# Attention rewritten in transposed form, two heads at a time, and issued between the feed-forward chunks

## The chip, the cores and the metric

One core of a Trainium2 chip. The metric is device time in microseconds (us) of one execution. Timed runs of a single core agree here within about 1.5%, and all times below are medians. Each profile is one execution, so its span differs by a few us from the timed runs. A ratio is the mean time of one kernel's fast runs over the mean of the other's of the same rounds, so it is not quite the ratio of the medians that are quoted.

## The reference, cut to what matters

```python
# q, k, v: (4 batches, 8 heads, 768 positions, 64), fp32
scores = (q @ k.T) / 8
keep = (column < 4) | ((row - column >= 0) & (row - column < 128))   # 4 sink keys, window 128
a = exp(scores where keep), each row divided by its sum
x = (a @ v) as (3072 tokens, 512)
out = (relu(x @ w_gate) * (x @ w_val)) @ w_out                        # 512 -> 1536 -> 512
```

## The kernel before

The attention handles one head and 128 queries at a time. Queries and keys are loaded as fp32 through SyncE and transposed on TensorE; v is loaded with a cast to bf16 by GpSimd, one load per head.

```python
for b in range(B):
    for h in range(H):
        nc.sync.dma_start(out=qL[:], in_=q[b, h].rearrange("(n p) d -> p n d", p=128))
        nc.sync.dma_start(out=kL[:], in_=k[b, h].rearrange("(n p) d -> p n d", p=128))
        for t in range(nqt):                       # 6 tiles, fp32 transposes of q and k
            nc.tensor.transpose(tp[:, :], qL[:, t, :], ident[:, :]); # ... copy, the same for k
        nc.gpsimd.dma_start(out=vA[:, :, :D], in_=v[b, h].rearrange("(n p) d -> p n d", p=128))
        for qt in range(nqt):
            # per key tile (sinks as a tile of 4): scores 128x128, Exp, mask, value matmul
            # then reciprocal, scale, fp32 transpose, copy, store to a temporary in memory
```

The feed-forward starts when all attention is done: it loads its weights, then per 256 tokens reloads the transposed attention from the temporary, and runs 12 steps of gate and value matmuls (256 columns) and 24 output matmuls (512 columns).

The softmax here doesn't subtract the row's maximum and nothing guards it: scores larger than these inputs give would overflow.

Of the kernel before, what the change touches and what calls it, by code (L numbers as in the profile page):

```python
# [8 lines left out]
F32 = mybir.dt.float32  # L9
BF16 = mybir.dt.bfloat16  # L10
Alu = mybir.AluOpType
Act = mybir.ActivationFunctionType


@with_exitstack
def kernel(
# [12 lines left out]
    nc = tc.nc  # L29
    B, H, S, D = q.shape  # L30
    n_sink = 4
    window = 128
    assert D == 64 and S % 128 == 0
    QT = 128
    nqt = S // QT
    scale = 1.0 / (D ** 0.5)

    d_model = moe_w_gate.shape[0]
    d_ff = moe_w_gate.shape[1]
    n_tokens = B * S  # L40
    assert d_model == H * D

    xT = nc.dram_tensor("xT_tmp", (d_model, n_tokens), F32, kind="Internal").ap()

    const = ctx.enter_context(tc.tile_pool(name="const", bufs=1))
    ident = const.tile([128, 128], F32)
    make_identity(nc, ident)

    m_causal_sink = const.tile([128, 128], BF16)
    m_strict_sink = const.tile([128, 128], BF16)  # L50
    m_causal = const.tile([128, 128], BF16)
    for m, op, cm, st in ((m_causal_sink, Alu.is_ge, -1, 1), (m_strict_sink, Alu.is_gt, 1, -1), (m_causal, Alu.is_ge, -1, 1)):
        nc.gpsimd.memset(m[:], 1.0)
        nc.gpsimd.affine_select(out=m[:], in_=m[:], compare_op=op, fill=0.0,
                                base=0, pattern=[[st, 128]], channel_multiplier=cm)
    nc.gpsimd.memset(m_causal_sink[0:n_sink, :], 1.0)
    nc.gpsimd.memset(m_strict_sink[0:n_sink, :], 1.0)
    m_strict = const.tile([128, 128], BF16)
    nc.gpsimd.memset(m_strict[:], 1.0)
    nc.gpsimd.affine_select(out=m_strict[:], in_=m_strict[:], compare_op=Alu.is_gt, fill=0.0,  # L60
                            base=0, pattern=[[-1, 128]], channel_multiplier=1)

    attn_ctx = ExitStack()
    qkpool = attn_ctx.enter_context(tc.tile_pool(name="qk", bufs=3))
    vpool = attn_ctx.enter_context(tc.tile_pool(name="vp", bufs=3))
    spool = attn_ctx.enter_context(tc.tile_pool(name="sp", bufs=4))
    ps_s = attn_ctx.enter_context(tc.tile_pool(name="ps_s", bufs=2, space=bass.MemoryType.PSUM))
    ps_av = attn_ctx.enter_context(tc.tile_pool(name="ps_av", bufs=2, space=bass.MemoryType.PSUM))
    ps_t = attn_ctx.enter_context(tc.tile_pool(name="ps_t", bufs=2, space=bass.MemoryType.PSUM))
    opool = attn_ctx.enter_context(tc.tile_pool(name="op", bufs=3))  # L70

    for b in range(B):
        for h in range(H):
            qL = qkpool.tile([128, nqt, D], F32)
            kL = qkpool.tile([128, nqt, D], F32)
            nc.sync.dma_start(out=qL[:], in_=q[b, h].rearrange("(n p) d -> p n d", p=128))
            nc.sync.dma_start(out=kL[:], in_=k[b, h].rearrange("(n p) d -> p n d", p=128))
            qT = qkpool.tile([D, nqt, 128], BF16)
            kT = qkpool.tile([D, nqt, 128], BF16)
            for t in range(nqt):  # L80
                tp = ps_t.tile([D, 128], F32)
                nc.tensor.transpose(tp[:, :], qL[:, t, :], ident[:, :])  # L82
                nc.vector.tensor_copy(qT[:, t, :], tp[:, :])  # L83
                tp = ps_t.tile([D, 128], F32)
                nc.tensor.transpose(tp[:, :], kL[:, t, :], ident[:, :])  # L85
                nc.vector.tensor_copy(kT[:, t, :], tp[:, :])  # L86
            vA = vpool.tile([128, nqt, D + 1], BF16)
            nc.gpsimd.dma_start(out=vA[:, :, :D], in_=v[b, h].rearrange("(n p) d -> p n d", p=128))  # L88
            nc.vector.memset(vA[:, :, D], 1.0)

            for qt in range(nqt):
                if qt == 0:
                    kts = [(0, 128, m_causal_sink)]
                elif qt == 1:
                    kts = [(0, 128, m_strict_sink), (1, 128, m_causal)]
                else:
                    kts = [(0, n_sink, None), (qt - 1, 128, m_strict), (qt, 128, m_causal)]

                av = ps_av.tile([128, D + 1], F32)
                first = True  # L100
                for ki, (ktidx, ksz, mask) in enumerate(kts):
                    s_ps = ps_s.tile([128, 128], F32)
                    nc.tensor.matmul(  # L103
                        out=s_ps[:ksz, :128],
                        lhsT=kT[:, ktidx, :ksz],
                        rhs=qT[:, qt, :],
                        start=True, stop=True,
                    )
                    e = spool.tile([128, 128], BF16)
                    nc.scalar.activation(e[:ksz, :], s_ps[:ksz, :], Act.Exp, bias=0.0, scale=scale)  # L110
                    if mask is not None:
                        nc.vector.tensor_tensor(e[:ksz, :], e[:ksz, :], mask[:ksz, :], op=Alu.mult)  # L112
                    last = ki == len(kts) - 1
                    nc.tensor.matmul(  # L114
                        out=av[:, :], lhsT=e[:ksz, :], rhs=vA[:ksz, ktidx, :],
                        start=first, stop=last,
                    )
                    first = False

                osb = opool.tile([128, D], F32)  # L120
                rcp = opool.tile([128, 1], F32)
                nc.vector.reciprocal(rcp[:, :], av[:, D:D + 1])  # L122
                nc.vector.tensor_scalar(osb[:, :], av[:, :D], rcp[:, :], None, op0=Alu.mult)  # L123
                ot_ps = ps_t.tile([D, 128], F32)
                nc.tensor.transpose(ot_ps[:, :], osb[:, :], ident[:, :])  # L125
                ot = opool.tile([D, 128], F32)
                nc.vector.tensor_copy(ot[:, :], ot_ps[:, :])  # L127
                nc.sync.dma_start(
                    out=xT[h * D:(h + 1) * D, b * S + qt * 128: b * S + qt * 128 + 128],
                    in_=ot[:, :],  # L130
                )

    attn_ctx.close()
    KI = 128
    ko_m = d_model // KI
    ff_m = d_ff // KI

    wpool = ctx.enter_context(tc.tile_pool(name="wpool", bufs=1))
    wg = wpool.tile([KI, ko_m, d_ff], BF16)
    wv = wpool.tile([KI, ko_m, d_ff], BF16)  # L140
    wo = wpool.tile([KI, ff_m, d_model], BF16)
    nc.gpsimd.dma_start(out=wg[:], in_=moe_w_gate.rearrange("(ko ki) n -> ki ko n", ki=KI))
    nc.gpsimd.dma_start(out=wv[:], in_=moe_w_val.rearrange("(ko ki) n -> ki ko n", ki=KI))
    nc.gpsimd.dma_start(out=wo[:], in_=moe_w_out.rearrange("(ko ki) n -> ki ko n", ki=KI))

    xpool = ctx.enter_context(tc.tile_pool(name="xpool", bufs=3))
    hpool = ctx.enter_context(tc.tile_pool(name="hpool", bufs=2))
    ps_g = ctx.enter_context(tc.tile_pool(name="ps_g", bufs=1, space=bass.MemoryType.PSUM))
    ps_o = ctx.enter_context(tc.tile_pool(name="ps_o", bufs=1, space=bass.MemoryType.PSUM))
    orpool = ctx.enter_context(tc.tile_pool(name="orpool", bufs=3))  # L150

    TOK = 256
    ntt = n_tokens // TOK
    TG = TOK // 128

    for tt in range(ntt):
        xt = xpool.tile([KI, ko_m, TOK], BF16)
        nc.gpsimd.dma_start(
            out=xt[:],
            in_=xT.rearrange("(ko ki) t -> ki ko t", ki=KI)[:, :, tt * TOK: (tt + 1) * TOK],  # L160
        )
        hT = hpool.tile([KI, ff_m, TOK], BF16)
        for m in range(ff_m):
            gp = ps_g.tile([KI, TOK], F32)
            vp = ps_g.tile([KI, TOK], F32)
            for ko in range(ko_m):
                nc.tensor.matmul(out=gp[:], lhsT=wg[:, ko, m * KI:(m + 1) * KI],  # L167
                                 rhs=xt[:, ko, :], start=ko == 0, stop=ko == ko_m - 1)
            for ko in range(ko_m):
                nc.tensor.matmul(out=vp[:], lhsT=wv[:, ko, m * KI:(m + 1) * KI],  # L170
                                 rhs=xt[:, ko, :], start=ko == 0, stop=ko == ko_m - 1)
            gs = hpool.tile([KI, TOK], F32)
            nc.scalar.activation(gs[:], gp[:], Act.Relu, bias=0.0, scale=1.0)  # L173
            nc.vector.tensor_tensor(hT[:, m, :], gs[:], vp[:], op=Alu.mult)  # L174
# [43 lines left out]
```

## Time and profile before

| | before |
|---|---|
| device time | 621.58 us (621.3 to 621.86) |
| TensorE busy | 565.2 us, 91% of the span |
| GpSimd busy | 40.3 us, 7% |
| attention, weight hole, feed-forward | about 390, 28 and 202 us |

A group's line in the profile gives the source line, the engine, the operation, what it writes and reads, the count, then busy us and mean ns of one, then the us that the engine sat idle just before these instructions and what ended most of that. The slices cut the span in 40 equal parts, each digit being the busy share in tenths. The lines themselves stand in the prediction.

### The profile page before, as it was taken

How to read it: one execution, taken by the hardware profiler on the slowest of the kernel's cores; microseconds unless marked ns; L12 is line 12 of the kernel's file. 1: busy time of each engine (PE TensorE's matmuls, PEld its weight loads, DVE VectorE, ACT ScalarE, POOL GpSimd, SP SyncE). 2: the span in 40 equal slices, each digit the busy share in tenths (PEclk: the TensorE clock that was granted, in tenths of full speed). 3: DMA queues.
4: the chain of work that ended last, by engine and by line, in shares of the span. 5: the costliest groups of instructions: out<-in, count | busy, mean ns of one | idle time of the engine just before them, and what ended most of it. 6: DMA issues, size and time to landing. Idle time of an engine off the chain costs nothing.

```text
span 619.8 us, 9768 instructions
## 1 busy us (share of the span) xinstructions
PE 565.2 (91%) x2976; PEld 299.5 (48%) x2976; DVE 331.2 (53%) x1512; ACT 185.8 (30%) x625; POOL 40.3 (7%) x63
## 2 busy tenths in 40 slices
PE   6899999999999999999999998069999999999996
PEld 2344444444444444444444444036667766666664
DVE  4666666666666666667666666113333433333332
ACT  3333333332333333333333333012222222222221
POOL 3100101010010001001000000100000000000000
PEclk9999999999999999999999999999999999999999
DMA  8333235533323323333332300692121122222000
GB/s 125 53 54 73 50 59 83 90 50 53 73 49 58 72 50 59 58 61 52 55 73 50 58 16 16 121 194 51 35 52 32 40 51 52 51 53 52 35 35 34
DMA packets 103075, 36.80 MB, mean 59 GB/s; under 512 B 78960, under 2 KB 98928, under 8 KB 103024
## 3 DMA queue, kind: packets, MB, share of 16 engines
q0 software_dynamic: 34032, 11.01, 16.6%
q1 hardware_dynamic: 68992, 25.18, 16.0%
q8 instruction: 23, 0.38, 0.3%
q14 instruction: 28, 0.23, 0.1%
HBM read 34.60 MB, written 12.58 MB: 76 GB/s over the span
## 4 chain that ended last, share of the span: by engine, by line
PE 80%; DVE 11%; DMA 5%; issue 2%; ACT 2%; POOL 0%; SPq 0%; POOLq 0%; DVEq 0%; ACTq 0%
PE s_ps L103 15%; PE vp L170 11%; PE op L178 10%; PE gp L167 10%; PE tp L82 10%; PE av L114 8%; PE ot_ps L125 8%; PE tp L85 7%; DMA wo<-in_moe_w_out_dram 4%; DVE qT L83 3%; DVE e L112 2%; DVE rcp L122 2%; DVE ot L127 2%; ACT e L110 2%; DVE kT L86 1%
## 5 line engine op out<-in xcount | busy, mean ns | idle before, releaser
L110 ACT ACTIVATE e<-s_ps 128x128 bf16<-128x128 f32 (+1 forms) x480 | 129.2, 275 | 256.4 <-PE s_ps L103 120.4
L103 PE MATMUL s_ps<-qT,kT 64*128 64x128 bf16 (+1 forms) x480 | 127.0, 275 | 2.8 <-ACT e L110 2.6
L174 DVE TENSOR_TENSOR hT<-gs,vp 128x256 bf16<-128x256 f32 x144 | 60.5, 420 | 115.4 <-PE vp L170 115.4
L173 ACT ACTIVATE gs<-gp 128x256 f32<-128x256 f32 x144 | 55.4, 384 | 168.2 <-PE gp L167 154.9
L167 PE MATMUL gp<-xt,wg 128*128 128x256 bf16 x576 | 88.4, 276 | 14.8 <-DMA wg<-in_moe_w_gate_dram 13.8
L114 PE MATMUL av<-vA,e 128*128 128x65 bf16 (+1 forms) x480 | 95.5, 239 | 6.3 <-DVE e L112 5.2
L82 PE MATMUL tp<-ident,qL 128*64 128x128 f32 x192 | 80.6, 420 | 15.6 <-DVE qT L83 8.4
L170 PE MATMUL vp<-xt,wv 128*128 128x256 bf16 x576 | 87.3, 274 | 4.0 <-DMA wv<-in_moe_w_val_dram 3.2
L178 PE MATMUL op<-wo,hT 128*128 128x512 bf16 x288 | 87.2, 379 | 2.0 <-DMA wo<-in_moe_w_out_dram 0.8
L85 PE MATMUL tp<-ident,kL 128*64 128x128 f32 x192 | 80.4, 419 | 4.6 <-DVE kT L86 0.9
L127 DVE COPY ot<-ot_ps 64x128 f32<-64x128 f32 x192 | 52.7, 280 | 47.7 <-PE ot_ps L125 43.9
L103 PEld LDWEIGHTS <-kT 64*128 64x128 bf16 (+1 forms) x480 | 44.6, 94 | 69.5 <-issue 49.1
L114 PEld LDWEIGHTS <-e 128*128 128x128 bf16 (+1 forms) x480 | 46.5, 106 | 61.9 <-issue 27.5
L170 PEld LDWEIGHTS <-wv 128*128 128x128 bf16 x576 | 56.0, 97 | 40.5 <-issue 26.8
L125 PE MATMUL ot_ps<-ident,osb 128*64 128x128 f32 x192 | 74.0, 419 | 0.8 <-DVE osb L123 0.8
L83 DVE CAST qT<-tp 64x128 bf16<-64x128 f32 x192 | 53.3, 277 | 32.8 <-PE tp L82 28.0
L167 PEld LDWEIGHTS <-wg 128*128 128x128 bf16 x576 | 56.9, 99 | 25.2 <-issue 16.0
L86 DVE CAST kT<-tp 64x128 bf16<-64x128 f32 x192 | 53.0, 276 | 23.0 <-PE tp L85 22.4
L123 DVE TENSOR_SCALAR osb<-av,rcp 128x64 f32<-128x64 f32 x192 | 50.9, 273 | 0.0
L82 PEld LDWEIGHTS tp<-ident,qL 128*64 128x64 f32 x192 | 24.6, 128 | 53.4 <-DVE qT L83 31.3
L88 POOL DMA_DIRECT2D vA<-in_v_dram x32 | 26.4, 824 | 317.7 <-DVE rcp L122 272.2
L122 DVE RECIPROCAL rcp<-av 128x1 f32<-128x1 f32 x192 | 31.2, 165 | 24.1 <-PE av L114 22.5
(30 smaller groups left out, 185.9 us busy)
## 6 DMA issues: line engine op xcount, KB each, us to landing
qL<-in_q_dram SPq DMA_DIRECT2D x32, 192.0 KB, 2.8
kL<-in_k_dram SPq DMA_DIRECT2D x32, 192.0 KB, 3.0
xT_tmp<-ot SPq DMA_DIRECT2D x192, 32.0 KB, 1.9
out_dram<-ot SPq DMA_DIRECT2D x24, 256.0 KB, 2.0
vA<-in_v_dram POOLq DMA_DIRECT2D x32, 96.0 KB, 3.3
xt<-xT_tmp POOLq DMA_DIRECT2D x12, 256.0 KB, 4.3
wg<-in_moe_w_gate_dram POOLq DMA_DIRECT2D x1, 1536.0 KB, 10.5
wv<-in_moe_w_val_dram POOLq DMA_DIRECT2D x1, 1536.0 KB, 17.1
```

What stands on the lines that cost most here:

```text
L82: nc.tensor.transpose(tp[:, :], qL[:, t, :], ident[:, :])
L83: nc.vector.tensor_copy(qT[:, t, :], tp[:, :])
L85: nc.tensor.transpose(tp[:, :], kL[:, t, :], ident[:, :])
L103: nc.tensor.matmul(out=s_ps[:ksz, :128], lhsT=kT[:, ktidx, :ksz], rhs=qT[:, qt, :], start=True, stop=True,)
L110: nc.scalar.activation(e[:ksz, :], s_ps[:ksz, :], Act.Exp, bias=0.0, scale=scale)
L114: nc.tensor.matmul(out=av[:, :], lhsT=e[:ksz, :], rhs=vA[:ksz, ktidx, :], start=first, stop=last,)
L125: nc.tensor.transpose(ot_ps[:, :], osb[:, :], ident[:, :])
L127: nc.vector.tensor_copy(ot[:, :], ot_ps[:, :])
L167: nc.tensor.matmul(out=gp[:], lhsT=wg[:, ko, m * KI:(m + 1) * KI], rhs=xt[:, ko, :], start=ko == 0, stop=ko == ko_m - 1)
L170: nc.tensor.matmul(out=vp[:], lhsT=wv[:, ko, m * KI:(m + 1) * KI], rhs=xt[:, ko, :], start=ko == 0, stop=ko == ko_m - 1)
L174: nc.vector.tensor_tensor(hT[:, m, :], gs[:], vp[:], op=Alu.mult)
L178: nc.tensor.matmul(out=op[:], lhsT=hT[:, m, tg * 128:(tg + 1) * 128], rhs=wo[:, m, :], start=m == 0, stop=m == ff_m - 1)
```

## The change

The intent is to take the attention off TensorE's time: fewer and wider matmuls, no fp32 transposes, no trip of the result through memory, and the attention of the next batch done between the feed-forward chunks of this one. Keys lie in tiles of 128; every second tile has the 4 sink keys in its first 4 rows and 124 keys of its own. Everything is loaded as bf16 with a cast during the load, tile by tile, through GpSimd. The value tile carries columns of ones, so the value matmul also gives the sums; these go through memory to be inverted in a compact layout and to come back broadcast. The core of the diff, with cuts marked by "...":

```diff
-            nc.sync.dma_start(out=qL[:], in_=q[b, h].rearrange("(n p) d -> p n d", p=128))
-            nc.sync.dma_start(out=kL[:], in_=k[b, h].rearrange("(n p) d -> p n d", p=128))
...
-            nc.gpsimd.dma_start(out=vA[:, :, :D], in_=v[b, h].rearrange("(n p) d -> p n d", p=128))
...
+ROW0 = [0, 124, 252, 376, 504, 628, 752]
...
+    def load_q(b, p, ts, slot):
+        for t in ts:
+            nc.gpsimd.dma_start(out=qn[slot][:, t, :, :], in_=rows(q, b, p, t * 128, 128))
+
+    def load_kv(b, p, js, slot):
+        for x, dst in ((k, kn[slot]), (v, vn[slot])):
+            for j in js:
+                r0 = ROW0[j]
+                lo, hi = (4, 128) if j in (1, 3, 5) else ((0, 16) if j == 6 else (0, 128))
+                nc.gpsimd.dma_start(out=dst[lo:hi, j, :, 0:64], in_=rows(x, b, p, r0 + lo, hi - lo))
+                if j in (1, 3, 5):
+                    nc.gpsimd.dma_start(out=dst[0:4, j, :, 0:64], in_=rows(x, b, p, 0, 4))
...
+    def st_T(s, qts, js):        # stage T: bf16 transposes of q and k of two heads, copies
...
+    def st_S(s, g):              # stage S: scores of up to 507 columns per head, Exp, mask
...
+    def st_V(s, half, oab):      # stage V: value matmuls with the sums, copy
...
+    def norm(b, p, oab, q0, n, d1, d2):
+        nc.sync.dma_start(out=dd.rearrange("(o h s) -> o h s", o=1, h=2), in_=oab[64:65, :, q0:q0 + n])
+        nc.sync.dma_start(out=dc[0:pp, 0:cc], in_=dd.rearrange("(p c) -> p c", c=cc))
...          # d1 chunks later: reciprocal, store, broadcast load; d2 later: two multiplies
+            for m in range(FM):
+                ci = bi * FM + m
+                want = (ci + 1) * 5 // 2 if ci < 17 else 42 + (ci - 16) * 24 // 24
+                while si < min(total, want):
+                    for L in load_at.pop(si, []):
+                        L()
+                    stages[si]()
+                    si += 1
+                tick()
+                chunk(b, c0, n, m)
```

A "pair" below is two heads of one batch, 16 in all; a full pair takes 26 loads: 12 of 128 rows, 6 of 124, 6 of 4 (the sinks) and 2 of 16. Batch 0 is done in halves, the first half of all four pairs before the first chunk. A "chunk" is one step of gate and value matmuls, 96 in all.

## The prediction

> **What bounds the kernel now.** I read the page first, then the chain of waits, then a table of stretches, then the groups by form. From the page:
>
> ```profile
> span 619.8 us, 9768 instructions
> PE 565.2 (91%) x2976; PEld 299.5 (48%) x2976; DVE 331.2 (53%) x1512; ACT 185.8 (30%) x625; POOL 40.3 (7%) x63
> ...
> PE   6899999999999999999999998069999999999996
> ...
> PE 80%; DVE 11%; DMA 5%; issue 2%; ACT 2%; POOL 0%; SPq 0%; POOLq 0%; DVEq 0%; ACTq 0%
> PE s_ps L103 15%; PE vp L170 11%; PE op L178 10%; PE gp L167 10%; PE tp L82 10%; PE av L114 8%; PE ot_ps L125 8%; PE tp L85 7%; DMA wo<-in_moe_w_out_dram 4%; DVE qT L83 3%; DVE e L112 2%; DVE rcp L122 2%; DVE ot L127 2%; ACT e L110 2%; DVE kT L86 1%
> ```
>
> TensorE is occupied nearly throughout, and the chain that sets the end is 80% TensorE. The slices show two phases with a hole between them, near 390 to 418 us: the wait for the feed-forward weights (their load is 4% of the chain). Two stretches tell the phases apart (columns: stretch, its length, then busy time and count of PE, PEld, DVE, ACT, POOL, then clock, DMA share, GB/s):
>
> ```profile
> 200.00:300.00 100.00, 93.58 (x401) 41.60 (x400) 66.72 (x352) 33.34 (x125) 6.54 (x8) 1.00 0.34 58
> 430.00:520.00 90.00, 89.97 (x644) 62.06 (x643) 33.66 (x75) 24.92 (x65) 3.70 (x5) 1.00 0.22 50
> ```
>
> In attention, TensorE starts only 4.0 matmuls per us, in the feed-forward 7.2, and those are the wider ones. So attention (about 390 us) is not arithmetic: it is many short matmuls and fp32 transposes, each separated by hand-offs. The feed-forward is dense. In the chain listed in order of time, the bursts of twelve output matmuls start at 445.19, 462.01 and 478.83 us: 16.82 us per 256 tokens, 202 us for twelve. Its columns are 12 x (96 x 256 + 24 x 512) = 442,368[...].
>
> The second thing to see is an engine that is idle now, GpSimd, because the change gives it work. The groups by form:
>
> ```profile
> L88 POOL DMA_DIRECT2D vA<-in_v_dram x32 | 26.4, 824 | 317.7 <-DVE rcp L122 272.2 <-PE av L114 22.3 <-PE s_ps L103 12.1
> L158 POOL DMA_DIRECT2D xt<-xT_tmp x12 | 8.9, 744 | 165.1 <-PE vp L170 160.5 <-DVE e L112 2.3 <-DMA xT_tmp<-ot 2.2
> L144 POOL DMA_DIRECT2D wo<-in_moe_w_out_dram x1 | 1.0, 1037 | 0.0
> L142 POOL DMA_DIRECT2D wg<-in_moe_w_gate_dram x1 | 0.8, 752 | 38.4 <-DMA xT_tmp<-ot 38.4
> ```
>
> One issue of a casting load takes GpSimd 0.74 to 1.04 us, hardly depending on bytes (256 KB and 1536 KB: both about 0.75). Two of them back to back show that this is occupancy and not latency:
>
> ```profile
> 4.10 1.66 POOL L88 DMA_DIRECT2D vA<-in_v_dram  x2
> ```
>
> [...] wo is 1.04 us on GpSimd and 24.4 us to landing. [...] in the changed kernel every q, k and v load, fp32 to bf16, is on that engine. In the kernel before, q and k go by SyncE. [...] Twelve output matmuls of N = 512 take 2.66 us in the chain, 222 ns each [...].
>
> **The change part by part.**
>
> *TensorE work.* Removed: 384 fp32 transposes of q and k (161 us busy), 192 of the output (74), 480 score matmuls (127), 480 value matmuls (95.5). Added per pair of heads and batch, 16 times: 13 bf16 transposes of 128 columns, 2 x 1417 score columns, 2 x 1417 value columns, in all 7,332 columns [...] my estimate is 3.9 us. Feed-forward: 96 chunks of 8 matmuls of about 384 columns [...], with 3 output matmuls each (0.67) [...]: 2.04 us per chunk, 96 x 2.04 = 196 us. Sum: 196 + 16 x 3.9 = 258 us. If TensorE alone bound it, with a prologue of some 50 us in place of part of the attention, and a tail of 10, the end would be near 305 us.
>
> *VectorE and ScalarE.* ScalarE rows give 278 ns at 128 elements and 384 at 256, so 0.83 ns per element: per pair 2.9 us of Exp, 0.9 of copies of kT, 1.6 of outputs, and 6 chunks x 0.49; with the output copies 9.3 us per pair. VectorE at about 1.05 ns per element (420 at 256): some 10 us. Both lie well below the 16 us that TensorE needs per pair (6 x 2.04 + 3.9), so both are beside it.
>
> *GpSimd.* Fit the four rows by contiguous source runs (v 768, xt 512, wo 1536, wg 512): 0.598 us + 0.29 ns per run fits all within 10 ns. A 128-row load of two heads has 256 runs: 0.67 us. A pair needs 26 loads: 18 big ones (18 x 0.67 = 12.06), 6 sink loads of 8 runs (3.6), 2 of 32 runs (1.2): 16.9 us. That is more than TensorE's 16. Splitting one load of 768 runs (0.82) into three or more is what costs.
>
> *The path that sets the end.* GpSimd in order: first halves of the four pairs of batch 0, 4 x 7.23, with 3.5 us of constants and start: 32 us. Eight weight quarters: issue 6 us, but the built program lets only eight loads be outstanding (each waits for the landing of the eighth before), and the weights, 4.7 MB in 24.4 us before, give 2.0 us per quarter; so the next eight loads wait, and GpSimd is 7 us late. Second halves 4 x 9.65: about 85 us. Output weights and their waits: 93 us. Then 12 pairs x 16.9 = 203: the last load is issued at 296 us less a little overlap, and lands 3.3 us later as v does now: T of the last pair starts near 297 us. In the changed program's order, 56 of the 96 chunks stand before it. After it: 40 chunks x 2.04 = 82 us, the last pair's attention 4 us, 36 output matmuls left at the end 8 us, a copy and a store 2.5 us. Sum: 297 + 96.5 = 393 us by trace.
>
> TensorE could not have been later: its chunks 0 to 55 and fourteen pairs are some 170 us of work after a start near 50 us. It waits for loads. The 28 us weight hole disappears in the prologue; the store of the transposed attention to memory and its reload vanish from the path too.
>
> **The rivals.**
>
> *A: loads cost less, TensorE binds.* If the fixed 0.6 us shrinks for small shapes, the steady state becomes TensorE's 16.1 us per pair and only the first part still waits for loads. For it: the fit is extrapolated from 512 runs down to 8. With 20% cheaper loads the third batch starts near 140 us, then 81 chunks x 2.04, 8 pairs x 3.9 and the tail give 348. With no waiting at all about 305.
>
> [...]
>
> *C: the transfers bind.* Between 100 and 380 us the casting queue shows 18,832 packets at 14.4% of 16 engines, 34 ns each. A pair has 4,672 runs, 292 per engine, 9.9 us: less than 16.9. It is hidden unless landing exceeds eight issues (5.4 us).
>
> *D: the normalisation round trip (four transfers of about 2 us on SyncE, with the VectorE waiting in order) stalls a chunk.* It is placed some five chunks (over 10 us) ahead; I give it a few us at most.
>
> **Range and chances.** The base sum is 393, halfway towards A pulls it down, B pushes it up; I take 386, range 340 to 420. A result over 600 would need the fixed cost of a load to double, so faster is nearly certain: 0.98.
>
> **What would show it.** Right: GpSimd busy 70% or more with DMA issues of about 0.67 us; TensorE busy under 75%, its largest idle before the transposes, released by loads of q (the last of each pair); the GpSimd work ending near 300 us, after which TensorE is dense; each late chunk 2.04 us. A is right if GpSimd has gaps and q is not what TensorE waits for; B if the 124-row issues are longer than the 128-row ones; C if loads take over 5.4 us to land and GpSimd waits for landings; D if the transposed output's multiply sits on the chain. The prediction is wrong above all if an issue of a small load costs much less, or more, than 0.6 us.

The feed-forward came to 2.04 us per chunk: 0.67 for the three output matmuls, from the 222 ns of the trace, and the rest in two terms. The 3.9 us for a pair of heads is like the 2.04 an estimate; the 16 us per pair, 258, 305, 348 and the 393 us of the whole are made with both. By the trace alone, the feed-forward before took 202 us for 442,368 columns, 2.19 columns per ns; at that rate a chunk of 4,608 columns takes 2.10 us and the 7,332 columns of a pair 3.35. Rival B was that the 124-row loads cost more than those of 128 rows; it came to 0.88 us for each and 413 us in all. The 1.05 ns per element of VectorE is an estimate as well: the groups by form give 165 ns at 1 element, 276 to 280 at 128 and 420 at 256, so 1.0 to 1.1 per element between them. The limit of eight outstanding loads can be seen in the trace of the changed kernel: after the eight weight loads (40.30 to 46.3 us), loads two to eight that follow wait 0.60 to 1.67 us each, for wv and wg in turn, and the ninth for a load of k.

## The result, and the profile after

The changed kernel takes 465.17 us (463.48 to 466.86) against 621.58: ratio 0.748, 95% interval 0.742 to 0.755. It is much faster, but 79 us slower than the 386 predicted, and outside the range of 340 to 420.

From the page of the changed kernel, the lines that answer to those of before:

```profile
span 465.0 us, 5011 instructions
PE 292.8 (63%) x1752; PEld 170.9 (37%) x1752; DVE 143.7 (31%) x280; ACT 140.8 (30%) x225; POOL 349.6 (75%) x439
...
PE   0033320564062818254959798897969699999996
...
POOL 8999499995999999999999999999999400000000
PEclk9999999988557676695979897989889799999999
...
POOL 61%; PE 23%; DMA 9%; issue 6%; ACT 0%; POOLq 0%; ACTq 0%
POOL vn L92 20%; POOL kn L92 17%; POOL qn L85 13%; PE op L265 8%; PE gp L246 7%; PE vp L252 7%; POOL vn L94 5%; POOL kn L94 4%; DMA kn<-in_k_dram 3%; DMA wo<-in_moe_w_out_dram 2%; DMA qn<-in_q_dram 2%; DMA vn<-in_v_dram 1%; PE ops L181 1%; POOL wg L99 1%; POOL wv L99 1%
```

TensorE's busy time fell from 565 to 293 us, so the work did go. But the chain that ended last was 80% TensorE and is now 61% GpSimd, all of it loads (L92, L94 and L85 load q, k and v, L99 the weights). GpSimd is nearly full for 31 slices but two, and where it stops TensorE becomes dense. The table of stretches says the same (stretch, length, then busy time and count of PE, PEld, DVE, ACT, POOL, clock, DMA share, GB/s):

```profile
86.00:365.00 279.00, 183.49 (x1145) 110.12 (x1145) 92.74 (x167) 96.64 (x148) 271.95 (x336) 0.81 0.68 62
365.00:465.00 100.00, 93.70 (x529) 51.60 (x528) 30.47 (x53) 32.59 (x60) 0.94 (x2) 0.97 0.15 45
```

Between 86 and 365 us GpSimd is busy 97% of the time, TensorE 66%. The groups by form show what a load costs, and what TensorE waits for:

```profile
L92 POOL DMA_DIRECT2D kn<-in_k_dram x112 | 107.4, 968 | 10.5 <-DMA wo<-in_moe_w_out_dram 4.8 <-DMA wv<-in_moe_w_val_dram 2.9 <-DMA wg<-in_moe_w_gate_dram 1.3
...
L85 POOL DMA_DIRECT2D qn<-in_q_dram x96 | 69.6, 744 | 1.8 <-DMA vn<-in_v_dram 1.1 <-issue 0.7
...
L94 POOL DMA_DIRECT2D kn<-in_k_dram x48 | 28.4, 591 | 1.2 <-DMA wg<-in_moe_w_gate_dram 0.6 <-DMA wv<-in_moe_w_val_dram 0.6
...
L144 PE MATMUL tps<-ident,qn 128*128 128x128 bf16 x96 | 23.0, 263 | 126.6 <-DMA qn<-in_q_dram 115.3 <-POOL ident masks.py:199 11.0
```

TensorE idles 115 us for q, which is the last load of each pair. GpSimd itself waits for almost nothing. L92 mixes forms, so its 968 ns is a mean; the GpSimd timeline in the steady part separates them (start, time, then the merged instructions):

```profile
254.11 4.34 POOL L85 DMA_DIRECT2D qn<-in_q_dram  x6
258.44 2.05 POOL L92 DMA_DIRECT2D kn<-in_k_dram  x2
260.48 0.60 POOL L94 DMA_DIRECT2D kn<-in_k_dram  x1
```

A 128-row load takes 4.34 / 6 = 0.72 us. The two of L92 are one of 128 and one of 124 rows, so the 124-row load takes 2.05 - 0.73 = 1.32 us, nearly twice as long for fewer bytes. A sink load of 4 rows takes 0.59. A pair thus takes 12 x 0.73 + 6 x 1.32 + 6 x 0.59 + 2 x 0.51 = 21.2 us of GpSimd; the chain shows the q loads of successive pairs starting at 127.0, 148.1, 169.2 and 190.3 us, a step of 21.1.

The granted clock was 0.81 on the mean of the stretch from 86 to 365 us. It does not set the pace there: GpSimd's waits, 16 us in the whole span, are for landings of earlier loads and for its own issue, none for TensorE. In the experiment "resident" below, where TensorE is dense from 110 us on, the clock is 0.98 to 1.00; when it falls is not worked out here. The 1.00 that the views show at the start of a run is no measurement. The clock entries of the trace begin at 90.0 us in the changed kernel, and the views count what lies before as full; yet four gate matmuls of 380 columns take 1.47 us at 87.23 and 0.80 at 92.54. In the kernel before, the entries begin only at 414.5 us: four of 256 columns take 1.04 us at 413.56 and 0.60 at 415.19. That its attention ran at a lowered clock as well is my estimate from these two times; no record shows it.

### The profile page after: what moved, and what is told of

Its sections match the earlier page's. It is cut to its first block, busy times and chain, and to the rows that moved or that the text cites. A ratio compares the mean times of both kernels' runs of the same rounds, so it can differ in the third digit from the quotient of the medians.

```text
span 465.0 us, 5011 instructions
## 1 busy us (share of the span) xinstructions
PE 292.8 (63%) x1752; PEld 170.9 (37%) x1752; DVE 143.7 (31%) x280; ACT 140.8 (30%) x225; POOL 349.6 (75%) x439
## 3 DMA queue, kind: packets, MB, share of 16 engines
q0 software_dynamic: 160944, 14.61, 47.5%
## 4 chain that ended last, share of the span: by engine, by line
POOL 61%; PE 23%; DMA 9%; issue 6%; ACT 0%; POOLq 0%; ACTq 0%
POOL vn L92 20%; POOL kn L92 17%; POOL qn L85 13%; PE op L265 8%; PE gp L246 7%; PE vp L252 7%; POOL vn L94 5%; POOL kn L94 4%; DMA kn<-in_k_dram 3%; DMA wo<-in_moe_w_out_dram 2%; DMA qn<-in_q_dram 2%; DMA vn<-in_v_dram 1%; PE ops L181 1%; POOL wg L99 1%; POOL wv L99 1%
## 5 line engine op out<-in xcount | busy, mean ns | idle before, releaser
L92 POOL DMA_DIRECT2D kn<-in_k_dram x112 | 107.4, 968 | 10.5 <-DMA wo<-in_moe_w_out_dram 4.8
L92 POOL DMA_DIRECT2D vn<-in_v_dram x112 | 107.0, 960 | 1.5 <-DMA wg<-in_moe_w_gate_dram 1.1
L252 PE MATMUL vp<-xT,wv 128*128 128x384 bf16 (+2 forms) x384 | 86.5, 352 | 1.2 <-ACT gs L249 1.2
L246 PE MATMUL gp<-xT,wg 128*128 128x384 bf16 (+2 forms) x384 | 85.7, 349 | 0.0
L254 DVE TENSOR_TENSOR hT<-gs,vp 128x384 bf16<-128x384 f32 (+2 forms) x96 | 52.4, 547 | 66.9 <-PE vp L252 66.2
L85 POOL DMA_DIRECT2D qn<-in_q_dram x96 | 69.6, 744 | 1.8 <-DMA vn<-in_v_dram 1.1
L249 ACT ACTIVATE gs<-gp 128x384 f32<-128x384 f32 (+2 forms) x96 | 47.2, 491 | 39.3 <-PE gp L246 38.8
L169 ACT ACTIVATE ee<-sps 128x1014 bf16<-128x1014 f32 (+3 forms) x52 | 45.6, 899 | 25.3 <-PE sps L166 25.2
L170 DVE TENSOR_TENSOR ee<-ee,msk 128x1014 bf16<-128x1014 bf16 (+3 forms) x52 | 31.7, 614 | 39.5 <-ACT ee L169 39.4
L181 PE MATMUL ops<-ee,vn 128*128 128x252 bf16 (+5 forms) x256 | 32.8, 278 | 17.1 <-DVE dr L223 9.2
```

Of the source, the lines that this page charges most:

```text
L85: nc.gpsimd.dma_start(out=qn[slot][:, t, :, :], in_=rows(q, b, p, t * 128, 128))
L92: nc.gpsimd.dma_start(out=dst[lo:hi, j, :, 0:64], in_=rows(x, b, p, r0 + lo, hi - lo))
L169: nc.scalar.activation(e, ps[:, :, lo:hi], Act.Exp, bias=0.0, scale=scale)
L181: nc.tensor.matmul(out=ps[:, h, o0:o0 + c1 - c0], lhsT=vn[s][:, j, h, :], rhs=ee[s][:, gi, h, c0:c1], start=i == 0, stop=i == len(segs) - ...
L246: nc.tensor.matmul(out=gp[:, 0:n], lhsT=wg[:, ko, m * 128:(m + 1) * 128], rhs=x[:, ko, c0:c0 + n], start=ko == 0, stop=ko == KO - 1)
L249: nc.scalar.activation(gs[:, 0:n], gp[:, 0:n], Act.Relu, bias=0.0, scale=1.0)
```

## The experiments

The theory after the result: the time in which GpSimd issues loads sets the pace, and the miss is the cost of one load, above all of a 124-row load. The rivals: the transfers themselves bind; TensorE, its clock, or the normalisation's round trips bind. Eleven kernels ran.

### Cheaper loads, slightly more bytes: rows128

```diff
-                lo, hi = (4, 128) if j in (1, 3, 5) else ((0, 16) if j == 6 else (0, 128))
-                nc.gpsimd.dma_start(out=dst[lo:hi, j, :, 0:64], in_=rows(x, b, p, r0 + lo, hi - lo))
+                hi = 16 if j == 6 else 128
+                nc.gpsimd.dma_start(out=dst[0:hi, j, :, 0:64], in_=rows(x, b, p, r0, hi))
...             # the loads of 4 sink rows come after q and write over rows 0 to 3
```

> The 124-row loads of the odd tiles become 128-row loads, and the 4 sink rows are written over them by the same tiny loads, issued after q. My theory after the result: GpSimd's time to issue loads sets the pace (it is occupied without a gap to 369 us), and a 124-row load costs 1.32 us there [...]. Then 96 loads fall from 1.32 to about 0.73 us, 57 us less: about 408 us, with GpSimd's work ending near 310 us. Rival, transfers bind: bytes rise by 3%, so 465 to 475 us and GpSimd gets gaps.

Measured: 410.8 us, ratio to the kernel before 0.661 (0.657 to 0.664), correct. The groups by line of this run:

```profile
L92 POOL DMA_DIRECT2D kn<-in_k_dram x112 | 78.0, 700 | 10.5 <-DMA wo<-in_moe_w_out_dram 3.1 <-issue 3.0 <-DMA wv<-in_moe_w_val_dram 2.4
```

The mean of L92 fell from 968 to 700 ns, GpSimd's busy time from 349.6 to 290.2 us, and the total by 54 us for 59 us of issue. The program asks for 3% more bytes and is faster. That alone does not clear the transfers, because the queue of GpSimd's loads moved far fewer packets, 90,288 where the changed kernel has 160,944 (the counts by shape are further down):

```profile
q0 software_dynamic: 90288, 14.42, 46.3%
```

What clears them is a kernel with as few packets and unchanged issue time: rows112_12, below, which takes 462.8 us.

### Dearer issue, hardly any bytes: extra_tiny

```diff
                     nc.gpsimd.dma_start(out=dst[0:4, j, :, 0:64], in_=rows(x, b, p, 0, 4))
+                    nc.gpsimd.dma_start(out=scratch[:, n_scr[0] % 16, :, :], in_=rows(x, b, p, 0, 4))
+                    n_scr[0] += 1
```

> Beside each of the 96 loads of 4 sink rows, a second one of the same size goes to a scratch tile that nobody reads. Bytes rise by 0.2% of the loads. Issue theory: 96 x 0.59 us = 57 us more, about 522 us. Transfer rival or a TensorE bound: at most 5 us more, about 467 us.

Measured: 522.3 us, ratio 0.840 (0.835 to 0.845), correct. The 96 tiny loads that nobody reads cost 57 us; their issue time, 579 ns each in the groups of this run, is 56:

```profile
L97 POOL DMA_DIRECT2D scratch<-in_v_dram x48 | 27.8, 579 | 0.0
```

TensorE waited 172 us for q, where it was 115. Packets rose by 2.9% only (165,552), the time by 12%. Together with rows128 and rows112_12 this shows the issue as the bound, from both sides.

### Loads of batches 1 to 3 left out: resident

```diff
                 def L(b=b, p=p):
-                    load_kv(b, p, range(7), p)
-                    load_q(b, p, range(6), p)
+                    pass
```

> Wrong on purpose: the loads of q, k and v for batches 1 to 3 are left out, the attention works on what batch 0 left in the tiles. It shows what remains when loads cost nothing after batch 0. Issue theory: the second halves of batch 0 and the output weights are issued as now near 104 us with chunk 4; then TensorE runs dense: 92 chunks x 1.95 us + 12 pairs x 3.9 us + 10 us of tail = 236 us, about 342 us in all, GpSimd idle after 105 us. If it stays above 400 us, something else than loads (the normalisation round trip, VectorE, the lowered clock) paces the later batches.

Measured: 350.7 us, ratio 0.564, and a wrong result, as intended. So loads after batch 0 are worth 114 us of the changed kernel. From 110 us on TensorE is dense, as two stretches of this run show:

```profile
110.00:200.00 90.00, 81.46 (x631) 53.89 (x638) 53.77 (x97) 54.57 (x82) 0.00 (x0) 0.98 0.24 57
200.00:300.00 100.00, 98.22 (x657) 60.09 (x668) 48.49 (x84) 48.77 (x82) 0.00 (x0) 1.00 0.18 54
```

Its clock is 0.98 to 1.00, and TensorE is idle for 10.3 of these 190 us. The run took 9 us more than expected.

### Which row counts are dear: rows112_12, rows120_4, rows122_2

Each 124-row load is cut in two, at different places, from the same first partition (4).

```diff
-                lo, hi = (4, 128) if j in (1, 3, 5) else ((0, 16) if j == 6 else (0, 128))
-                nc.gpsimd.dma_start(out=dst[lo:hi, j, :, 0:64], in_=rows(x, b, p, r0 + lo, hi - lo))
+                for lo, hi in (((4, 116), (116, 128)) if j in (1, 3, 5) else (((0, 16),) if j == 6 else ((0, 128),))):
+                    nc.gpsimd.dma_start(out=dst[lo:hi, j, :, 0:64], in_=rows(x, b, p, r0 + lo, hi - lo))
```

The other two put the cut at 124 (120 rows and 4) and at 126 (122 rows and 2).

> Each 124-row load (partitions 4 to 127) is cut into 112 rows from partition 4 and 12 rows. Theory, the count of rows sets the cost (124 is not a multiple of 16): the 112-row load issues in about 0.70 us and the 12-row load in about 0.55, 1.25 together against 1.32: about 458 us. Rival, the start at partition 4 is what costs: the 112-row load stays at 1.2 us or more, the 12-row load comes on top, about 520 us.

> Each 124-row load is cut into 120 and 4 rows. [...] 120 rows [...] issue in about 0.72 us, the 4 rows in 0.59: 1.31 against 1.32, total about 463 us. If instead every count that is no multiple of 16 is slow, the 120-row load takes 1.2 us or more and the total is above 510 us.

> Each 124-row load is cut into 122 and 2 rows. [...] about 2.0 us of issue, plus 0.58 for the 2 rows, so 96 x 1.26 = 121 us more, about 585 us. If only the multiple of 16 matters, 122 rows cost 1.3 us as 124 do, and the total is about 520 us.

Measured, one run each (so of unknown state), all correct: 462.8, 470.0 and 586.5 us, where 458, 463 and 585 were expected. (The last two forecasts rested on a view of how a load's rows are spread that no trace shows; their 0.72 and 2.0 us stand as estimates.) The start at partition 4 is not what costs, nor is a count that is no multiple of 16: 120 rows are cheap. 122 rows are dearest. In the GpSimd timeline of the run with 120 + 4 rows and of that with 122 + 2 rows, one 128-row load and one cut pair:

```profile
244.70 2.08 POOL L92 DMA_DIRECT2D kn<-in_k_dram  x3 [0.48 <-issue]
```

```profile
241.43 3.31 POOL L92 DMA_DIRECT2D vn<-in_v_dram  x3
```

With 0.73 for the 128-row load and 0.55 to 0.59 for the small piece, 120 rows take about 0.77 us and 122 rows about 2.0. In the run with 112 + 12 rows the same three loads take 1.99 us, so 112 rows take about 0.68. A load of 112, 120 or 128 rows thus took 0.68 to 0.77 us, one of 124 rows 1.32 and one of 122 rows 2.0. Why is not shown.

The packet counts differ in the same way. The lines of the queue that carries GpSimd's loads, of the changed kernel, of 112 + 12, of 120 + 4 and of 122 + 2 rows (packets, MB, share of 16 engines):

```profile
q0 software_dynamic: 160944, 14.61, 47.5%
```

```profile
q0 software_dynamic: 91824, 14.33, 40.8%
```

```profile
q0 software_dynamic: 94896, 14.34, 40.5%
```

```profile
q0 software_dynamic: 257712, 15.00, 45.5%
```

The 90,288 packets of rows128, further up, are fewer than any of these. For each of the 96 places where the changed kernel has a 124-row load, 112 + 12 rows bring 16 more, 120 + 4 rows 48, the 124 rows 736, and 122 + 2 rows 1,744: the dear shapes are those with many more packets. By size, 74,752 of the packets in the trace of the changed kernel are of 128 bytes, as many as q, k and v have runs there (16 x 4,672), 5,632 are larger, as many as the weights have, and the other 80,560 are of 4 bytes; in the kernel before, 752 of 34,032 are of 4 bytes. (A run is a stretch of source data that lies together in memory: here the 64 numbers of one row of one head.) What the packets of 4 bytes are for, and whether they are what takes GpSimd's time, is not shown.

The same counts test the transfers as the bound. The run with 112 + 12 rows has 43% fewer packets than the changed kernel but nearly the same GpSimd time (343.3 us for 349.6), and it takes 462.8 us for 465.2: the time follows the issue and not the packets.

### One part undone: serial

All attention stages are issued before the first chunk; the loads stay as they are.

```diff
         total = len(stages)
+        while si < total:      # xT buffers 4 for 2, output buffers 2 for 3
+            for L in load_at.pop(si, []):
+                L()
+            stages[si]()
+            si += 1
+            tick()
+        flush()
```

> One part of the change undone: all attention stages first, then all feed-forward chunks (buffers of the transposed output doubled to 4, output buffers 2 instead of 3); loads as in the changed kernel. Issue theory: the attention still ends when the loads do, near 370 us, and the 96 chunks x 1.95 us + 10 us of tail follow bare: about 567 us. So the interleaving would be worth some 100 us of the gain of 156. Rival, interleaving does not matter because TensorE is the bound: about 465 us.

Measured: 577.7 us, ratio 0.930 (0.926 to 0.933), correct. The stretches of this run, before and after the loads end:

```profile
0.00:365.00 365.00, 118.45 (x657) 74.60 (x658) 84.86 (x173) 79.40 (x98) 349.36 (x439) 1.00 0.67 56
...
375.00:575.00 200.00, 187.10 (x1045) 102.49 (x1043) 57.09 (x101) 60.72 (x119) 0.00 (x0) 0.97 0.09 34
```

(The clock of 1.00 in the first line is no measurement: the entries of this trace begin at 372.8 us. The other execution, 0.3% longer, has a mean of 0.757.) The loads end at nearly the same time as in the interleaved kernel. TensorE is busy 118 us of these 365, where the attention of the kernel before kept it busy 359 of 390: the new attention is a third of the work, and most of that saving is lost to loads. So of the 156 us gained, about 112 are the interleaving, which hides feed-forward chunks behind the loads, and 44 are all else.

### The late first chunk: after_n

In the changed kernel the first gate matmul starts at 87 us, where I had predicted about 50. SyncE's own timeline shows the normalisation of one pair, its four small transfers in a row:

```profile
45.06 0.71 SPq L217 DMA_DIRECT2D den_tmp<-oab  x1
50.14 0.30 SPq L219 DMA_DIRECT2D dc<-den_tmp  x1
55.66 0.25 SPq L224 DMA_DIRECT2D rcp_tmp<-dr  x1
60.20 0.69 SPq L226 DMA_DIRECT2D R<-rcp_tmp  x1
```

Each waits for the one before, about 5 us a step while the weights move, and the queue takes the next pair only then. In this experiment the four pairs go phase by phase.

```diff
-        def V0(p):
-            o = new_oab()
-            st_V(p, 0, o)
-            norm(0, p, o, 0, QCUT, 2, 2)
+        def V0(p):               # value matmuls and the store of the sums only
...
+        def norm_all():          # then: all loads of the sums; all reciprocals and stores;
...                              # broadcast loads and multiplies, two pairs at a time
```

> Only the normalisation of the first halves of batch 0 is reordered in the changed kernel: the four pairs' small transfers are issued phase by phase instead of pair by pair, so that the four round trips overlap and VectorE's mask multiplies do not queue behind them. The first chunk should start 20 to 30 us earlier (86 us in the changed kernel). Issue theory: the loads still set the end, so the total stays within 1% of 465 us. Rival: the late first chunk is on the path, then 440 to 445 us.

Measured: 463.8 us, ratio 0.747 (0.743 to 0.750), beside 0.748 without it. The first gate matmul in the changed kernel, and in this run:

```profile
87.23 1.47 PE L246 MATMUL gp<-xT,wg 128*128 128x380 bf16 x4
```

```profile
74.76 1.47 PE L246 MATMUL gp<-xT,wg 128*128 128x380 bf16 x4
```

The first chunk came 12.5 us earlier (20 to 30 were expected) and the total did not move. My prologue was wrong by nearly 40 us, and it did not matter.

### A version that beats both: merged, merged_w, merged_n

```diff
-        for t in ts:
-            nc.gpsimd.dma_start(out=qn[slot][:, t, :, :], in_=rows(q, b, p, t * 128, 128))
+        t0, n = ts[0], len(ts)
+        for h in range(2):
+            nc.gpsimd.dma_start(out=qn[slot][:, t0:t0 + n, h, :],
+                                in_=q[b, 2 * p + h, t0 * 128:(t0 + n) * 128, :].rearrange("(n p) d -> p n d", p=128))
...          # k and v: per head, tiles 0, 2, 4 in one load of 128 rows, tiles 1, 3, 5 in another
+                nc.vector.tensor_copy(kn[s][0:4, j, :, :], kn[s][0:4, 0, :, :])      # sinks, in stage T
+                nc.vector.tensor_copy(vn[s][0:4, j, :, 0:64], vn[s][0:4, 0, :, 0:64])
```

merged_w spreads the weight loads between those of batch 0's second halves; merged_n is merged with the reordering of after_n.

> All in one for the loads: q one load per head (6 tiles, 768 runs), k and v per head and parity of the tile (128 rows x 3 tiles, 384 runs), sink rows copied by VectorE from tile 0 (same partitions) in place of 96 tiny loads: 12 loads per pair in place of 26. Same bytes within 3%. Issue theory: 2 x 0.82 + 8 x 0.72 + 2 x 0.51 = 8.4 us of GpSimd per pair against 21.1; GpSimd is off the path, what is left is the prologue and dense TensorE: below the 351 us that the kernel without later loads took, since the first loads are shorter too (about 62 in place of 104 us of issue before batch 1): about 333 us. Transfer rival: 12.6 us of all 16 engines per pair stays, so above 400 us if transfers were pacing.

> As merged, but the eight gate and value weight quarters are not loaded in one burst: quarter 1 before the second halves of pair 0, quarter 2 before those of pair 1, and so on. In the changed kernel TensorE's first chunk starts near 86 us, not 50 as predicted: VectorE waits in order for the small transfers of the normalisation while 6 MB of weights move. If the weights delay those transfers, the first chunk starts about 15 us earlier and the total falls by 8 to 15 us against merged: about 322 us. If not, within 3 us of merged.

> The same reordering in the kernel with merged loads, where GpSimd no longer paces. The first chunk starts at 74.6 us there; with the round trips overlapped it should start near 53 us. If the prologue is on the path now, the total falls from 361 us by 10 to 20 us, about 346 us; if the transfers of the loads (all 16 engines full between 60 and 160 us) pace instead, it stays within 1% of 361 us.

Measured, all correct: merged 361.6 us, ratio 0.582 (0.576 to 0.588); merged_w 369.6 us, 0.595 (0.592 to 0.597); merged_n, in another set of runs, 358.8 us, 0.579 (0.575 to 0.583). Merging removes 104 us, less than I expected (333): GpSimd's busy time falls from 349.6 to 168 us, but a new wait comes. A stretch of merged_n:

```profile
60.00:160.00 100.00, 71.92 (x536) 47.03 (x541) 54.24 (x144) 49.25 (x72) 91.93 (x127) 0.90 1.13 102
```

Here the DMA share is 1.13, where it was 0.68 in the changed kernel between 86 and 365 us: now that issue is quick, the engines that move the data look full (the share adds up the times of packets, which overlap, so it can pass 1). GpSimd is busy 92 of these 100 us as well, but no wait of TensorE in this stretch is put down to a load of q, k or v. TensorE waits 40 us in all for VectorE's copies of the sink keys, and VectorE stands in order behind the small transfers of the normalisation. The line of waits of merged_n (us, times, longest), and the longest wait in its VectorE timeline:

```profile
PE tps L162 <- DVE kn L107: 40.1, 14, 10.7
```

```profile
83.57 0.20 DVE L238 RECIPROCAL dr<-dc 97x8 f32<-97x8 f32 x1 [9.53 <-DMA dc<-den_tmp]
```

All of VectorE's waits for these transfers sum to about 50 us. That the full engines are what makes them slow is my guess (VectorE waited 9.5 us for a transfer of 3 KB); no run separates it. The weights spread out made it slower, not faster, and I did not find out why; the sets of merged and merged_n overlap, so the reordering is within 1%. After 210 us TensorE is busy 137 of 145 us in merged_n: there it is TensorE that binds.

## Why the prediction was wrong

**What held.** GpSimd's issue as the new bound, TensorE waiting for q as the last load of each pair, GpSimd full until the last load and dense TensorE after it. From the landing of the last q load (367.6 us) to the end are 97.4 us; the prediction had 96.5. That this agrees so well is in part luck. The late chunks run at 1.95 us, so 40 of them are 3.6 us shorter than predicted, but the first matmuls after the wait ran at a clock of 0.50 (from 368 to 373 us) and the last copy and store took 3.6 us for 2.5. In the timeline from 400 to 412 us four matmuls of 384 columns take 0.65 us from start to start, four more the same, and three of 512 the same, 1.95 in all. VectorE and ScalarE stayed beside it, at 31% and 30%.

**The step that failed** is the term "18 x 0.67 = 12.06" in the sum of a pair's loads, 16.9 us. It measured 12 x 0.73 and 6 x 1.32, and the pair 21.1 us. That is 4.2 us per full pair, 50 us over 12 pairs; batch 0's pairs took 8.9 for 7.23 and about 12.3 for 9.65, another 17. The 67 us are nearly all of the 72 between my sum (393) and the trace (465). Of the 4.4 us per pair that the single times add up to, 3.9 come from the 124-row loads alone. The two 16-row loads and the sinks were about right.

**Why it was mis-sized.** I fitted a straight line through four loads, none of 124 rows, and used it for that shape too. I saw the other possibility and called it rival B, but sized it at 0.88 us per 124-row load, by an argument that no trace shows; it is 1.32. I left it half out of the number, and let rival A, which no run supported, pull the number down from 393 to 386. The 128-row load was 0.06 us dearer than the line as well.

**Rivals.** A was wrong: the small shapes here took 0.51 us or more. C was wrong for this kernel (43% fewer packets at equal issue left the time as it was, in rows112_12). D was right in the prologue (87 us for 50) and off the path, as the unchanged time of after_n shows; once the loads are merged, waits of D's kind are most of what is left between 60 and 210 us (TensorE waits 30 us there for VectorE's copies of the sinks, and about 1 to 2 us for anything else).

**A reading that does not hold.** The prediction says that hand-offs separate the matmuls of the old attention. In its own line, TensorE was idle only 6.4 of 100 us there, and the clock of 1.00 beside it was not measured; a lowered clock is a rival that it does not weigh. The sum of loads does not rest on either.

**Not settled.** When the clock falls, why merged_w is slower than merged, how far full transfer engines hold the merged kernels, and why loads of 124 and 122 rows take GpSimd so much longer than those of 112, 120 and 128.

## What to carry to other kernels

A casting load occupied GpSimd for 0.51 to 2.0 us here, 0.51 for 16 rows of two heads and 0.59 for 4, so when a rewrite splits loads, count them times their issue time and compare with the engine that the rewrite relieves. Measure the row count of such a load before settling on it (112 rows took about 0.68 us, 120 rows 0.77 and 128 rows 0.73, but 124 rows 1.32 and 122 rows 2.0): loading 4 rows too many and writing over them saved 54 us here. Before an overlap is credited to the faster work, undo it alone: of 156 us, 112 came from hiding work behind a bound that the rewrite itself had made.
